# A SwiGLU kernel whose first loads are dealt anew over two DMA queues, with ScalarE's table load ahead of its own

## The chip, the core and the metric

The kernel runs on one core of one Trainium2 chip. The metric is the device time of one execution in microseconds (us). Before the change, three timed runs took 120.75, 120.0 and 120.8 us, median 120.75. One further execution was profiled.

Five engines appear in what follows. TensorE (PE) does matmuls; its weight loads have a row of their own (PEld). VectorE (DVE), ScalarE (ACT) and GpSimd (POOL) do elementwise work. SyncE (SP) here only issues DMAs and waits. DMAs can be issued by SyncE and by ScalarE; each of the two has a queue of its own (q1 and q10 in the profile).

## What is computed

```
def reference(x, w_gate, w_up, w_down):
    g = _silu(x @ w_gate)
    u = x @ w_up
    return (g * u) @ w_down
```

All arrays are bfloat16: x is 1 x 2048 x 512 (tokens by D), w_gate and w_up are 512 x 1376 (D by F), w_down is 1376 x 512.

## The kernel before

The work has two phases. In the first, for each chunk of 512 tokens and each of the ten full tiles of 128 columns of F, PE computes a gate group and an up group (`gu_matmuls`, four matmuls each over D = 4 x 128); ScalarE applies SiLU to the gate group in PSUM and VectorE multiplies it with the up group. The 96 columns that are left over go through groups of their own (X and Y). In the second phase PE multiplies the result with w_down, ScalarE and VectorE copy it out of PSUM, and SyncE stores it.

PE needs x with D on the partitions (`xT_sb`). Tokens 0 to 255 of the first chunk come as plain loads (`load_xn`, tiles xn0 and xn1 of 128 tokens) and are transposed on PE (line 367); VectorE and ScalarE copy the transposes to `xT_sb` in turn (even and odd parts of D). Tokens 256 to 511 come by two DMA transposes (x0b, x0c), and the later chunks by one each (x1 to x3). The weights come in slabs of tiles: tile 0, tile 1, tiles 2-3, tiles 4-6, tiles 7-10, each with a load for gate (wg0, wg1, wg2, wg4, wg7) and one for up (wu0 ... wu7). "Ups 2-3" below is the load wu2.

The order of all this is written out by hand. Each engine has one stream of instructions; a DMA issue is an instruction in the stream of the engine that issues it, and each load has a semaphore of its own. ScalarE's stream (`on_scalar`) begins with gate 0 and xn1, then a dummy SiLU on four elements (line 277), ahead of which the program has a load of ScalarE's function table; then come its real operations, of which the first are copies of the transposes. SyncE's stream (`on_sync`) issues xn0, up 0, gate 1, up 1, gates 2-3, ups 2-3, x0b, x0c, and then all the rest.

PE's stream begins with seven matmuls on constants (`warm`: five of 512 columns and two of 128). Behind them stand:

- the four transposes of xn0, two more matmuls on constants, and gate tile 0 on tokens 0-127;
- the four transposes of xn1, up tile 0 on tokens 0-127, and gate and up tile 0 on tokens 128-255;
- tiles 1, 2 and 3 on tokens 0-255 in the order gate 1, up 1, gate 2, gate 3, up 2, up 3, as matmuls of 256 columns;
- tile 0 on tokens 256-383 and then on 384-511, tiles 1 to 3 on tokens 256-511, and from tile 4 on whole chunks of 512 columns.

Each waits for the semaphores of the loads that it uses (`need`) and for the copies (`after`).

Of the kernel before, what the change touches and what calls it, by code (L numbers as in the profile page):

```python
# [4 lines left out]
ACT = mybir.ActivationFunctionType  # L5
# [9 lines left out]
def bass_standalone__swiglu_ffn__prompt_kernel(nc, x, w_gate, w_up, w_down, out):  # L15
# [35 lines left out]
    with ExitStack() as es:  # L51
# [11 lines left out]
        adummy = sb("act_dummy", [P, 8], FP32)  # L63
# [21 lines left out]
        def load_sem(name):  # L85
            loads[name] = sem(f"s_{name}")
            return loads[name]
# [3 lines left out]
        zero_c = nc.const_aps.tensor(0.0, [P, 4], FP32)  # L91


        def load_x(eng, name, t0, t1):
            eng.dma_start_transpose(
                xT_sb[:, :, t0:t1], xf[t0:t1, :]
            ).then_inc(load_sem(name), 16)

        def load_w(eng, name, src, base, f0, f1):
            eng.dma_start(  # L100
                w_sb[:, :, base + f0:base + f1],
                src[:, f0:f1].rearrange("(k p) f -> p k f", p=P),
            ).then_inc(load_sem(name), 16)

        slabs = [(0, 1), (1, 2), (2, 4), (4, 7), (7, NFT)]
        slab_of = {ft: a for a, b in slabs for ft in range(a, b)}

        def load_gate(eng, a, b):
            load_w(eng, f"wg{a}", w_gate, 0, a * P, min(b * P, F))

        def load_up(eng, a, b):
            load_w(eng, f"wu{a}", w_up, UPH, a * P, min(b * P, F - 32))

        def load_xn(eng, i):
            eng.dma_start(xn_sb[:, i, :], xf[i * P:(i + 1) * P, :]).then_inc(load_sem(f"xn{i}"), 16)
# [2 lines left out]
            return of[t * P:(t + 1) * P, :]  # L118

        def loads_on_scalar(act):  # L120
            load_gate(act, *slabs[0])
            load_xn(act, 1)

        def loads_on_sync(sp):
            load_xn(sp, 0)
            load_up(sp, *slabs[0])
            for a, b in slabs[1:3]:
                load_gate(sp, a, b)
                load_up(sp, a, b)
            load_x(sp, "x0b", HT, HT + P)  # L130
            load_x(sp, "x0c", HT + P, SC)
            for a, b in slabs[3:]:
                load_gate(sp, a, b)
                load_up(sp, a, b)
            load_w(sp, "wut", w_up, F - (F - 32), F - 32, F)
            for c in range(1, NSC):
                load_x(sp, f"x{c}", c * SC, (c + 1) * SC)
            sp.dma_start(
                wd_sb[:, 0:NFF, :], w_down[0:NFF * P, :].rearrange("(k p) d -> p k d", p=P)
            ).then_inc(load_sem("wd"), 16)  # L140
            load_sem("wdt")
            for y0 in (0, 64):
                sp.dma_start(wd_sb[y0:y0 + 64, T01, :], w_down[NFF * P:F - SR, :]).then_inc(loads["wdt"], 16)
            for x0 in range(0, P, SR):
                sp.dma_start(wd_sb[x0:x0 + SR, T2, :], w_down[F - SR:F, :]).then_inc(loads["wdt"], 16)
            sp.dma_start(wd_sb[0:F_LAST, TAIL, :], w_down[NFF * P:F, :]).then_inc(load_sem("wdl"), 16)
# [104 lines left out]
        def ready(op):  # L251
            return op["ready"] if "ready" in op else (s_P, op["g"]["at"] + 1)

        def store_tiles(eng, own):
            for o, t, c0, c1, ob, copied, n in stores:
                if o == own:
                    eng.wait_ge(s_A if copied == "A" else s_D, n)
                    eng.dma_start(out_rows(t)[:, c0:c1], o_sb[ob][:, c0:c1]).then_inc(s_out[ob], 16)

        def on_sync(sp):  # L260
            loads_on_sync(sp)
            store_tiles(sp, "S")
            for i in range(NOS):
                sp.wait_ge(s_out[i], 16 * n_store[i])
# [9 lines left out]

        def on_scalar(act):
            loads_on_scalar(act)
            act.activation(adummy[:, 0:4], zero_c, ACT.Silu)  # L277
            for op in act_ops:
                act.wait_ge(*ready(op))
                if op["kind"] == "silu":  # L280
                    if op["free"]:
                        act.wait_ge(s_D, op["free"])
                    fn = ACT.Silu
                else:
                    if op["stored"][1]:
                        act.wait_ge(*op["stored"])
                    fn = ACT.Copy
                act.activation(op["out"], op["src"], fn).then_inc(s_A, 1)  # L288
            store_tiles(act, "A")
# [199 lines left out]
        on_sync(nc.sync)  # L489
        on_gpsimd(nc.gpsimd)  # L490
        on_scalar(nc.scalar)
        on_tensor(nc.tensor)
        on_vector(nc.vector)
# [28 lines left out]
```

## Time and profile before

| What | Value |
|---|---|
| timed runs | 120.0, 120.75, 120.8 us (median 120.75) |
| profiled execution, its time | 120.41 us |
| profiled execution, its span | 119.1 us, 2344 instructions |
| PE busy | 116.5 us, 98% of the span |
| VectorE, ScalarE busy | 38.3 and 35.2 us (32% and 30%) |
| DMA queue q1 (SyncE) | 16816 packets, 8.33 MB |
| DMA queue q10 (ScalarE) | 816 packets, 0.36 MB |

The span is the time from the first to the last instruction of the program in the profile; the execution's own time has 1.3 us more around it. In the lines shown further on, "0.74 0.46 ACTq L100 DMA_DIRECT2D w_sb<-in_w_gate_dram x1" means: at 0.74 us of the span the instruction stream of ScalarE issued a DMA for 0.46 us, by line 100, from w_gate to w_sb. A q behind an engine's name marks its instruction stream. In the table of DMA issues the last column is the time from the issue to the landing of the data. In the chain of waits each line has a start, a length, and the engine, tile and line that the chain goes through. PE's matmuls overlap each other, so the pace is read from their starts.

### The profile page before, as it was taken

The page shows a single profiled execution, that of the slowest core. Times are in us where ns is not written, and L with a number is a line of the kernel's source. Part 1 is how long each engine was busy: PE and PEld are TensorE (multiplying, and loading weights), DVE is VectorE, ACT ScalarE, POOL GpSimd, SP SyncE. Part 2 cuts the span into 40 slices and gives each one's busy share as a digit, 9 for nine tenths or more (in the row PEclk, how much of TensorE's full clock was granted, in tenths as well). Part 3 has the DMA queues.
Part 4 walks back from the last instruction along what each step waited for, and adds up shares of the span by engine and source line. Part 5 has one row for each costly group of instructions (what it writes and reads, how often), then busy time and mean ns, then how long its engine had stood idle before and what let it go on. Part 6 is the DMA issues. An engine that isn't in the chain of part 4 may idle for free.

```text
span 119.1 us, 2344 instructions
## 1 busy us (share of the span) xinstructions
PE 116.5 (98%) x1019; PEld 60.6 (51%) x1019; DVE 38.3 (32%) x61; ACT 35.2 (30%) x62; POOL 1.0 (1%) x7
## 2 busy tenths in 40 slices
PE   7999999999999999999999999999999999999993
PEld 2899544444444444444444444444444445885452
DVE  0204633444334444334453344361000044003321
ACT  3406444262343272442353432430000033003021
POOL 1000000000000000000000000001000000000000
DMA  4999989991000000000000000000000017200612
GB/s 84 296 176 347 265 178 239 265 340 29 0 6 0 0 0 0 0 6 0 0 0 6 0 0 0 0 0 6 0 6 0 0 51 235 77 0 6 204 61 88
DMA packets 17642, 8.83 MB, mean 74 GB/s; under 512 B 10624, under 2 KB 17632, under 8 KB 17632
## 3 DMA queue, kind: packets, MB, share of 16 engines
q1 hardware_dynamic: 16816, 8.33, 27.5%
q10 hardware_dynamic: 816, 0.36, 1.1%
q8 instruction: 8, 0.13, 0.4%
q14 instruction: 2, 0.02, 0.1%
HBM read 4.75 MB, written 2.10 MB: 58 GB/s over the span
## 4 chain that ended last, share of the span: by engine, by line
PE 98%; DVE 0%; issue 0%
PE bank L326 62%; PE bank L444 25%; PE bank L483 7%; PE bank L358 2%; PE bank L406 2%; PE bank L367 1%; DVE o_sb L302 0%
## 5 line engine op out<-in xcount | busy, mean ns | idle before, releaser
L326 PE MATMUL bank<-xT_sb,w_sb 128*128 128x512 bf16 (+2 forms) x384 | 73.7, 356 | 0.0
L326 PEld LDWEIGHTS bank<-xT_sb,w_sb 128*128 128x128 bf16 x384 | 37.0, 100 | 36.3
L298 DVE TENSOR_TENSOR hT_sb<-sg_sb,bank 128x512 bf16<-128x512 f32 x40 | 27.5, 687 | 40.5 <-PE bank L326 39.6
L288 ACT ACTIVATE sg_sb<-bank 128x512 f32<-128x512 f32 x40 | 23.8, 596 | 40.9 <-PE bank L326 40.8
L444 PE MATMUL bank<-wd_sb,hT_sb 32*128 32x512 bf16 x496 | 29.0, 374 | 0.0
L444 PEld LDWEIGHTS bank<-wd_sb,hT_sb 32*128 32x128 bf16 x496 | 15.2, 93 | 11.6 <-issue 0.4
L302 DVE CAST o_sb<-bank 128x512 bf16<-128x512 f32 (+1 forms) x10 | 5.7, 595 | 31.1 <-PE bank L444 25.9
L288 ACT ACTIVATE o_sb<-bank 128x512 bf16<-128x512 f32 (+1 forms) x8 | 4.3, 582 | 33.6 <-PE bank L444 27.9
L483 PE MATMUL bank<-wd_sb,hT_sb 128*128 128x512 bf16 (+2 forms) x56 | 8.1, 304 | 0.0
L483 PEld LDWEIGHTS bank<-wd_sb,hT_sb 128*128 128x128 bf16 x56 | 4.2, 97 | 4.2 <-issue 0.4
L444 PE MATMUL bank<-wd_sb,hy_sb 32*128 32x512 bf16 (+1 forms) x32 | 5.0, 371 | 0.0
L298 DVE TENSOR_TENSOR hx_sb<-sgx_sb,bank 32x512 bf16<-32x512 f32 x4 | 2.8, 692 | 3.5 <-ACT sgx_sb L288 3.5
L288 ACT ACTIVATE sgx_sb<-bank 32x512 f32<-32x512 f32 x4 | 2.3, 587 | 4.5 <-PE bank L326 4.5
L358 PE MATMUL bank<-const-bfloat16-1.0 128*128 128x512 bf16 (+1 forms) x9 | 2.9, 486 | 0.8 <-PEq L507 0.8
L444 PE MATMUL bank<-wd_sb,hx_sb 32*128 32x512 bf16 (+1 forms) x16 | 3.0, 371 | 0.0
L288 ACT ACTIVATE sgy_sb<-bank 64x512 f32<-64x512 f32 x4 | 2.4, 590 | 0.1
L358 PEld LDWEIGHTS bank<-const-bfloat16-1.0 128*128 128x128 bf16 x9 | 1.1, 140 | 2.1 <-issue 2.1
L406 PE MATMUL bank<-xT_sb,w_sb 128*64 128x512 bf16 x16 | 1.9, 382 | 0.0
L444 PEld LDWEIGHTS bank<-wd_sb,hy_sb 32*128 32x128 bf16 x32 | 1.6, 93 | 0.6
L302 DVE COPY xT_sb<-bank 128x128 bf16<-128x128 bf16 x4 | 0.9, 224 | 3.0 <-PE bank L367 3.0
L277 ACT ACT_TABLE_LOAD x1 | 1.3, 1283 | 1.8 <-issue 1.8
L406 PEld LDWEIGHTS bank<-xT_sb,w_sb 128*64 128x64 bf16 x16 | 0.8, 109 | 1.0 <-DVE hT_sb L298 0.4
(16 smaller groups left out, 7.3 us busy)
## 6 DMA issues: line engine op xcount, KB each, us to landing
out_dram<-o_sb SPq DMA_DIRECT2D x15, 128.0 KB, 1.8
wd_sb<-in_w_down_dram SPq DMA_DIRECT2D x1, 1280.0 KB, 8.3
w_sb<-in_w_gate_dram SPq DMA_DIRECT2D x1, 480.0 KB, 5.5
w_sb<-in_w_up_dram SPq DMA_DIRECT2D x1, 448.0 KB, 7.5
w_sb<-in_w_gate_dram SPq DMA_DIRECT2D x1, 384.0 KB, 4.0
w_sb<-in_w_up_dram SPq DMA_DIRECT2D x1, 384.0 KB, 4.4
w_sb<-in_w_up_dram SPq DMA_DIRECT2D x2, 128.0 KB, 3.3
w_sb<-in_w_gate_dram SPq DMA_DIRECT2D x1, 256.0 KB, 3.7
```

The lines of the kernel that those rows point to most:

```text
L277: act.activation(adummy[:, 0:4], zero_c, ACT.Silu)
L288: act.activation(op["out"], op["src"], fn).then_inc(s_A, 1)
L298: ins = dve.tensor_tensor(op["out"], op["a"], op["b"], ALU.mult)
L302: ins = dve.tensor_copy(op["out"], op["src"])
L326: return pe.matmul(bank[:, n0:n1], lhsT=w_sb[:, dk, col:col + P], rhs=xT_sb[:, dk, c * SC + n0:c * SC + n1], start=(dk == 0), stop=(dk == ...
L358: pe.matmul(banks[NB - 1][:, 0:width], lhsT=ones_w, rhs=ones_m[:, 0:width], start=True, stop=True)
L367: pe.matmul(tview(i, dk), lhsT=xn_sb[:, i, dk * P:(dk + 1) * P], rhs=ident[:, :], start=True, stop=True, is_transpose=True,).then_inc(s_X, 1)
L406: ins = pe.matmul(g["bank"][y0:y1, :], lhsT=w_sb[:, dk, YC0:YC0 + 64], rhs=xT_sb[:, dk, c * SC:(c + 1) * SC], start=(dk == 0), stop=(dk == ...
L444: ins = pe.matmul(g["bank"][:, 0:c1 - c0], lhsT=h, rhs=wd_sb[r0:r0 + SR, w, c0:c1], start=(start and fk == fks[0]), stop=(stop and fk == f ...
L483: ins = pe.matmul(g["bank"][:, 0:c1 - c0], lhsT=h, rhs=w, start=(last and fk == 0), stop=(fk == (NFF if last else NFF - 1)), skip_group_ch ...
```

## The change

ScalarE's dummy SiLU, with its table load, moves to the head of ScalarE's stream. Behind it, ScalarE issues gate 0 and xn1 as before, and now also up 1 and ups 2-3, which leave SyncE's stream. SyncE's order becomes xn0, up 0, gate 1, gates 2-3, x0b, x0c, and the rest as before. PE's, VectorE's and GpSimd's streams are the same.

```diff
         def loads_on_scalar(act):
+            act.activation(adummy[:, 0:4], zero_c, ACT.Silu)
             load_gate(act, *slabs[0])
             load_xn(act, 1)
+            for a, b in slabs[1:3]:
+                load_up(act, a, b)
 
         def loads_on_sync(sp):
             load_xn(sp, 0)
             load_up(sp, *slabs[0])
             for a, b in slabs[1:3]:
                 load_gate(sp, a, b)
-                load_up(sp, a, b)
             load_x(sp, "x0b", HT, HT + P)
             load_x(sp, "x0c", HT + P, SC)
...
         def on_scalar(act):
             loads_on_scalar(act)
-            act.activation(adummy[:, 0:4], zero_c, ACT.Silu)
             for op in act_ops:
```

## The prediction

> **What bounds the kernel now.** I read the page's parts 1 and 4 first, then the chain of waits cut to the first 12 us, the timeline of the loading stage, the table of DMA issues, and the windows. The chain of the whole span:
>
> ```profile
> PE 98%; DVE 0%; issue 0%
> ```
>
> TensorE (PE) is the path from 0.77 us to the end. The change touches only loads that land in the first 9 us, so what counts is whether PE waits for one of them. The chain of the first 12 us:
>
> ```profile
> 0.77 2.51 PE bank L358 x7
> 3.28 0.01 issue
> 3.29 0.58 PE bank L367 x4
> 3.88 0.21 PE bank L358 x2
> 4.09 0.46 PE bank L326 x4
> 4.55 0.47 PE bank L367 x4
> 5.01 7.01 PE bank L326 x73
> ```
>
> The seven warm-up matmuls fill the time until the first tokens (xn0) are there; then the work follows without a hole. What it follows on is seen from the issues (start, length of the issue) and from the time that each takes to land:
>
> ```profile
> 0.74 0.46 ACTq L100 DMA_DIRECT2D w_sb<-in_w_gate_dram  x1
> 0.74 0.40 SPq L115 DMA_DIRECT2D xn_sb<-in_x_dram  x1
> ...
> 1.23 0.53 ACTq L115 DMA_DIRECT2D xn_sb<-in_x_dram  x1
> ...
> 1.79 1.28 ACT L277 ACT_TABLE_LOAD   x1 [1.79 <-issue]
> ...
> 2.75 0.51 SPq L100 DMA_DIRECT2D w_sb<-in_w_gate_dram  x1
> ...
> 3.08 0.20 ACT L277 ACTIVATE act_dummy<-const-float32-0.0 128x4 f32<-128x4 f32 x1
> ...
> 3.30 0.51 SPq L100 DMA_DIRECT2D w_sb<-in_w_up_dram  x1
> ...
> 3.85 2.64 SPq L95 DMA_TRANSPOSE xT_sb<-in_x_dram  x2
> ```
>
> ```profile
> w_sb<-in_w_gate_dram SPq DMA_DIRECT2D x1, 256.0 KB, 3.7
> w_sb<-in_w_up_dram SPq DMA_DIRECT2D x1, 256.0 KB, 3.9
> w_sb<-in_w_gate_dram ACTq DMA_DIRECT2D x1, 128.0 KB, 2.9
> xn_sb<-in_x_dram SPq DMA_DIRECT2D x1, 128.0 KB, 2.4
> xn_sb<-in_x_dram ACTq DMA_DIRECT2D x1, 128.0 KB, 3.1
> ```
>
> Issue plus time to land gives the arrivals; beside them, from narrow cuts of PE's timeline, the first matmul that needs each. xn0: 0.74 + 2.4 = 3.1, used 3.29. Gate 0: 0.74 + 2.9 = 3.6, used 3.96 (set by the copies of the transposes, of which ScalarE's first starts at 3.70). xn1: 1.23 + 3.1 = 4.3, used 4.41: this one is only just in time. Gate 1: 1.66 + 3.4 = 5.1, used 6.06. Up 1: 2.20 + 3.3 = 5.5, used 6.50. Gates 2-3: 2.75 + 3.7 = 6.45, used 6.93. Ups 2-3: 3.30 + 3.9 = 7.2, used 7.81. Tokens 256-383 and 384-511: 7.9 and 8.3, used 8.68 and 9.13. So every load that the change moves is early by 0.5 to 1.0 us, and only xn0 and xn1 are on the path. One more thing is in these starts: up to 5.98 a 128-column matmul follows the last after 0.107 us, from 8.68 on after 0.056. PE runs at half pace for its first 5.2 us (0.77 to 5.98) and at full pace behind that. The granted clock in the windows stands at 1.00 in both, so the pace is read from the starts.
>
> **The change, part by part.** The sum is made against the profiled execution: span 119.1, time 120.41. The shown median is 120.75, so 0.34 above it; I add the same steps to both.
>
> (1) Table load and dummy SiLU ahead of ScalarE's two loads. They are 1.28 + 0.20 us of ScalarE's own work. The question is whether the instruction stream behind them, which now begins with four DMA issues, has to wait. Lower bound: only two instructions more to hand over. The nearest rows are two semaphore instructions of ScalarE 0.087 us apart (109.248 and 109.335), and SyncE's 0.05 to 0.06 between the end of an issue and the next; so 0.12 to 0.2 for both. Upper bound: all of 1.28 to 1.49. Two rows bear on it. The trace has the semaphore instruction at 109.335, which belongs to the copy that starts at 113.26, before the preceding copy has begun (109.74) and while the one before that runs (109.24 to 109.84): the stream goes on while the engine works. And the dummy starts 0.01 us after the table load's end (1.79 + 1.28 = 3.07, then 3.08), while VectorE shows 0.044 from a released semaphore instruction to the start of the work behind it: the dummy had been handed over while the table was loading. Both rows are of engine instructions and none is of a DMA behind a table load, so it stays a rival; I take the lower bound, 0.15. [...]
>
> With 0.15, gate 0 lands at 3.75, still ahead of 3.96: hidden by the copies, cost 0. xn1 lands near 4.5, so its transposes go from 4.41 to about 4.55. That is 0.15 of half-pace time; if full pace still comes at 5.98, the work left over runs twice as fast, so 0.07 to 0.15. I take 0.1. Against this, xn0 has the DMA engines to itself a little longer; it can gain at most 3.29 - 3.08 = 0.2 (where the warm-up ends), and I keep -0.1 as the lower end of this part.
>
> (2) Ups 1 and 2-3 leave SyncE's queue for ScalarE's. SyncE's later issues, gates 2-3 and all behind, come 0.55 earlier, from the tokens on 1.10 earlier (two issues of 0.51 with their gaps). Nothing waits for that: the tokens were 0.8 early. ScalarE issues four times, about 0.5 us each, from 0.9 to 3.1, and its next work is the copy at 3.70: cover of 0.6. The bytes to move by 7.2 are unchanged, and the DMA engines already run full then (286 to 303 GB/s in the windows 5:6 and 6:7). What changes is who shares: the two queues have 640 KB each up to gates 2-3 and ups 2-3, and at half the rate each they end about together, instead of at 6.45 and 7.2. Gates 2-3 are needed at 6.93. Bounds: 0, if their queue is ahead by the 0.15 of part (1) and by xn0's head start; 7.2 - 6.93 = 0.3, if they land only with ups 2-3. I take 0.05, near the lower end, because the head start is some 60 KB of 640 and the matmuls have moved back by 0.1 as well.
>
> (3) The table load is over at 2.0 and not 3.07. ScalarE's first real work waits for PE until 3.70; worth 0.
>
> Sum: +0.1 + 0.05 = +0.15: 120.56 against the profiled time, 120.9 against the median. Own range: -0.1 to +0.45, so 120.65 to 121.2, and with the runs' own spread (120.0 to 120.8) 120.0 to 121.3.
>
> **Rivals.** Rival 1, slower: the DMA issues wait for the table load. It decides as soon as ScalarE's first issue is later than about 0.74 + (3.96 - 3.6) = 1.1 us. Place: PE before its first real matmul. First issue 0.74 + 1.28 = 2.03, at most 2.24. Gate 0 lands at 2.03 + 2.9 = 4.9 to 5.1, xn1 1.3 to 1.5 late at 5.6 to 5.8. PE idles from 3.88 to 5.0 and again until 5.7. The four ScalarE copies come late too (issues until 4.2), behind gate 0. What it costs depends on the pace. If full pace still comes at 5.98: by then the old kernel had 1.57 us of half-pace time since 4.41, worth 0.79 at full pace; the new one has 0.28, worth 0.14; plus up to 0.1 for copies. That makes +0.7. If the idle time starts the 5.2 us of half pace anew at 5.0 to 5.6, full pace comes at 10.2 to 10.8; 5.2 us from 5.6 are then worth 2.6, against 0.79 + 4.8 = 5.6 in the old kernel: +3.0. So 121.1 to 123.4 against the profiled time, 121.45 to 123.75 against the median, middle 122.6. For it: no row shows a DMA of ScalarE behind a table load. Against it: the two rows of part (1). Chance 0.44, high for that evidence because everything hangs on one unseen order of two instructions, and the slack is 0.1 to 0.4 us.
>
> Rival 2: the tokens' transposes, 1.10 earlier, run between ups 2-3 of the other queue. Where transposes and copies follow each other now, the DMA engines slow down: 156 and 80 GB/s in the windows 7:8 and 8:9, against 286 in 6:7. If ups 2-3 land with the tokens at 8.3, PE waits 8.3 - 7.81 = 0.5: 121.3 against the median. Against it: at 6 to 7 us the two kinds overlap already, at 286 GB/s. Chance 0.06.
>
> Rival 3: xn0's gain of 0.1 to 0.2 outweighs the rest, 120.6. Against it: xn1 is the next to be waited for. Chance 0.05.
>
> **How the numbers follow.** My forecast, that the order on ScalarE costs next to nothing and the rest is hidden, has 0.45; predicted time 120.9. The range goes from the lowest run, 120.0, to 123.0, which takes in all but rival 1's upper quarter or so (0.13) and a little below (0.03). A measurement of this kernel tells about 1% from no change: below 119.55 or above 121.95. Rival 1 lies above that but for its lower fifth or so (0.37 of 0.44), rival 2 with 0.01: slower 0.38. Faster by 1% would need 1.2 us out of a PE that has only 0.2 us of waits in its head; 0.03 is left for it. The rest, 0.59, is within 1%.
>
> **What would show it.** Step (1) is right if ScalarE's first DMA issue stands near 0.9 while the table load still runs, and wrong if it stands at 2.0 or later. Step (2) is right if PE's first 256-column matmul stands near 6.1 and the chain has no wait at gates 2-3, near 7.0. Step (3) shows in ScalarE's first copy, still near 3.7. The prediction is wrong if PE has a hole between 3.9 and 5.7, and by how much is seen from the time at which the spacing falls from 0.107 to 0.056.

## The result, and the profile after

The changed kernel takes 120.97 us (median of 22 runs, 120.42 to 123.09). In the same series the kernel before takes 120.44 (22 runs, 119.94 to 120.8). The ratio is 1.0049, 95% interval 1.0034 to 1.0064: about 0.6 us slower, inside the 1% that was called "no change", and clear of zero. One of the changed kernel's 22 runs (123.09) was a slow one, and the ratios here and below leave slow runs out.

The profiled execution of the changed kernel has a span of 119.8 us and a time of 121.1. The chain of waits over the whole span no longer begins with PE (columns: start, length, what):

```profile
0.74 0.39 SPq L115
...
1.19 0.42 SPq L100
...
1.66 0.50 SPq L100
...
2.21 5.33 DMA w_sb<-in_w_gate_dram
7.54 0.05 issue
7.58 71.05 PE bank L327 x360
78.63 1.85 PE bank L407 x16
80.48 29.41 PE bank L445 x540
109.89 8.06 PE bank L484 x58
```

The path to the end now goes through one load, gates 2-3: issued by SyncE at 2.21, landed at 7.54, first matmul at 7.58. Behind that, nothing has changed: from the first matmul on gate 2 to the end of the span it is 112.18 us here (119.767 - 7.585) and 112.15 before (119.081 - 6.933). So the whole difference lies ahead of this matmul. PE's timeline there (the bracket gives idle time before the group and what ended it):

```profile
3.91 0.51 PE L327 MATMUL bank<-xT_sb,w_sb 128*128 128x128 bf16 x4
4.71 0.40 PE L368 MATMUL bank<-ident,xn_sb 128*128 128x128 bf16 x4 [0.29 <-DMA xn_sb<-in_x_dram]
4.94 0.94 PE L327 MATMUL bank<-xT_sb,w_sb 128*128 128x128 bf16 x12
6.15 1.06 PE L327 MATMUL bank<-xT_sb,w_sb 128*128 128x256 bf16 x8 [0.27 <-DMA w_sb<-in_w_gate_dram]
7.58 0.61 PE L327 MATMUL bank<-xT_sb,w_sb 128*128 128x256 bf16 x4 [0.38 <-DMA w_sb<-in_w_gate_dram]
```

PE waits three times: for xn1, for gate 1 and for gates 2-3. In this execution full pace came early, between 4.19 and 4.71 us (5.98 in the profile before), which gave PE time that it then spent waiting. Over all profiles here full pace comes anywhere from about 4.2 to 6.5, so the starts of two single profiles are not quite like with like. The fastest runs tell more: the fastest of 22 took 119.94 before and 120.42 after, so the best case moved by nearly as much as the median did. ScalarE's timeline shows the part that the prediction was least sure of:

```profile
0.74 1.28 ACT L121 ACT_TABLE_LOAD   x1 [0.74 <-PEq L508]
0.81 0.44 ACTq L100 DMA_DIRECT2D w_sb<-in_w_gate_dram  x1
1.28 0.53 ACTq L115 DMA_DIRECT2D xn_sb<-in_x_dram  x1
1.84 0.46 ACTq L100 DMA_DIRECT2D w_sb<-in_w_up_dram  x1
2.04 0.20 ACT L121 ACTIVATE act_dummy<-const-float32-0.0 128x4 f32<-128x4 f32 x1
2.32 0.53 ACTq L100 DMA_DIRECT2D w_sb<-in_w_up_dram  x1
```

The DMA issues run on while the table load (0.74 to 2.02) is under way, the first of them 0.07 us behind its start. The table of DMA issues tells where the time went instead (last column: from issue to landing):

```profile
w_sb<-in_w_gate_dram SPq DMA_DIRECT2D x1, 256.0 KB, 5.3
w_sb<-in_w_up_dram ACTq DMA_DIRECT2D x1, 256.0 KB, 5.8
...
xn_sb<-in_x_dram ACTq DMA_DIRECT2D x1, 128.0 KB, 3.4
w_sb<-in_w_gate_dram SPq DMA_DIRECT2D x1, 128.0 KB, 4.4
w_sb<-in_w_up_dram ACTq DMA_DIRECT2D x1, 128.0 KB, 4.7
```

Gates 2-3 are issued 0.54 earlier and take 5.3 us instead of 3.7. Gate 1 takes 4.4 instead of 3.4, up 1 4.7 instead of 3.3, ups 2-3 5.8 instead of 3.9. In landings: gate 1 6.10 (5.03 before), up 1 6.54 (5.47), gates 2-3 7.54 (6.43), ups 2-3 8.13 (7.21).

A load's semaphore gets 16 increments in the trace (those of gates 2-3 come from 5.73 to 6.43 before and from 5.72 to 7.54 after), and PE waits for the last of them. The trace has the time of each and names no DMA engine with it. For gates 2-3 the eighth comes at 6.00 before and 6.50 after, the last at 6.43 and 7.54. So the eighth is 0.5 later, and the last falls back by another 0.6. The DMA engines together move little less than before: 225 GB/s against 273 from 4 to 5 us, then 314 and 291 against 303 and 286 in the two windows behind it.

### The profile page after: what moved, and what is told of

It reads as the page before. It is cut to its first block, busy times and chain, and to the rows that moved or that the text cites. A ratio compares the mean times of both kernels' runs of the same rounds, so it can differ in the third digit from the quotient of the medians.

```text
span 119.8 us, 2344 instructions
## 1 busy us (share of the span) xinstructions
PE 116.2 (97%) x1019; PEld 59.7 (50%) x1019; DVE 38.3 (32%) x61; ACT 35.1 (29%) x62; POOL 1.0 (1%) x7
## 4 chain that ended last, share of the span: by engine, by line
PE 92%; DMA 4%; SPq 1%; issue 0%; DVE 0%
PE bank L327 59%; PE bank L445 25%; PE bank L484 7%; DMA w_sb<-in_w_gate_dram 4%; PE bank L407 2%; SPq L100 1%; SPq L115 0%; DVE o_sb L303 0%
## 5 line engine op out<-in xcount | busy, mean ns | idle before, releaser
L327 PEld LDWEIGHTS bank<-xT_sb,w_sb 128*128 128x128 bf16 x384 | 36.1, 98 | 37.6 <-DMA w_sb<-in_w_gate_dram 1.1
L289 ACT ACTIVATE xT_sb<-bank 128x128 bf16<-128x128 bf16 x4 | 0.9, 276 | 2.3 <-PE bank L368 2.3
```

The lines of the kernel that those rows point to most:

```text
L327: return pe.matmul(bank[:, n0:n1], lhsT=w_sb[:, dk, col:col + P], rhs=xT_sb[:, dk, c * SC + n0:c * SC + n1], start=(dk == 0), stop=(dk == ...
```

## The experiments

The theory with which they were begun, an assumption of the author's at that point: both queues share the DMA engines, so ups on ScalarE's queue take a share from the gates on SyncE's that PE uses sooner (sharing). Rivals: the table load (T), the tokens' transposes, issued earlier (X), two busy queues as such (Q), and a cost for any load that is moved (S). Each kernel's ratio is to the kernel before on the same chip. "Eighth" is the eighth of the 16 increments of gates 2-3 (in the run with halves the 16th of 32), "start" the first matmul on gate 2, "rest" the span less that start. The run with wide loads, whose gates come in one load, is told in its own section. All but the ratio are from one profile each.

| Kernel | ratio, 95% interval | gate 1 lands | gates 2-3: eighth, last | start | rest |
|---|---|---|---|---|---|
| before | 1 | 5.03 | 6.00, 6.43 | 6.93 | 112.15 |
| the change | 1.0049 (1.0034 to 1.0064) | 6.10 | 6.50, 7.54 | 7.58 | 112.18 |
| table load first, alone | 0.9999 (0.9982 to 1.0015) | 5.05 | 6.10, 6.35 | 6.52 | 112.15 |
| ups moved, alone | 1.0040 (1.0021 to 1.0060) | 5.26 | 6.23, 6.85 | 7.22 | 112.17 |
| halves on both queues | 1.0010 (0.9993 to 1.0028) | 5.40 | 5.84, 6.50 | 7.07 | 112.16 |
| transposes wait for xn1 | 1.0030 (1.0014 to 1.0047) | 5.77 | 6.35, 7.25 | 7.29 | 112.16 |
| transposes wait for gates 2-3 | 1.0202 (1.0187 to 1.0218) | 6.05 | 6.43, 7.44 | 7.49 | - |
| only up 1 moved | 1.0025 (1.0007 to 1.0044) | 5.67 | 6.13, 6.75 | 7.35 | 112.15 |
| only gate 1 moved | 1.0049 (1.0023 to 1.0074) | 6.64 | 6.35, 6.92 | 7.57 | 112.16 |
| only ups 2-3 moved | 1.0083 (1.0055 to 1.0111) | 5.74 | 7.62, 7.65 | 7.69 | 112.17 |
| mirrored: gates moved | 1.0090 (1.0064 to 1.0116) | 6.42 | 7.67, 7.87 | 7.91 | 112.17 |
| 928 KB more beside | 1.0328 (1.0281 to 1.0376) | 6.79 | 8.70, 9.50 | 9.55 | 113.66 |
| xn1 sooner | 1.0007 (0.9990 to 1.0023) | 5.25 | 6.23, 6.51 | 6.56 | 112.18 |

### The table load first, alone

```diff
         def loads_on_scalar(act):
+            act.activation(adummy[:, 0:4], zero_c, ACT.Silu)
             load_gate(act, *slabs[0])
             load_xn(act, 1)
...
             loads_on_scalar(act)
-            act.activation(adummy[:, 0:4], zero_c, ACT.Silu)
```

> The kernel before with the dummy SiLU and its table load moved ahead of ScalarE's two loads, and nothing else. Theory (the cost is the two queues' sharing of the DMA engines once the ups go to ScalarE): ScalarE's first DMA issue stands at 0.81 us while the table load runs, gates 2-3 land near 6.4 as before, PE does not wait for them, ratio to the kernel before 0.998 to 1.002. Rival T (the table load delays gate 0 and xn1, and all behind): xn1 lands at 4.5 or later, PE waits 0.1 to 0.3 us ahead of its transposes, ratio 1.002 to 1.005. Rival X (the tokens' transposes, issued earlier, slow the other loads): as the theory, since SyncE's order is unchanged.

Ratio 0.9999, ScalarE's first issue at 0.80, gates 2-3 at 6.35. PE does wait for xn1, as rival T said, and the chain of its first 13 us shows it:

```profile
0.73 0.50 ACT L121
1.23 0.03 issue
1.26 3.30 DMA xn_sb<-in_x_dram
4.57 0.05 issue
4.61 0.43 PE bank L367 x4
```

But the time is the same. xn1 was on the path before too (4.36, used 4.41), and 0.2 us of waiting there is within what the runs spread (119.97 to 120.72). T falls as a cause.

### The ups moved, alone

```diff
             load_gate(act, *slabs[0])
             load_xn(act, 1)
+            act.activation(adummy[:, 0:4], zero_c, ACT.Silu)
+            for a, b in slabs[1:3]:
+                load_up(act, a, b)
```

(with SyncE's side as in the change)

> The changed kernel with the dummy SiLU behind ScalarE's gate 0 and xn1 and ahead of its two ups: the ups' move alone. Theory: gates 1 and 2-3 land near 6.1 and 7.5 (5.0 and 6.4 in the kernel before), the first matmul on gate 2 starts near 7.6, ratio 1.003 to 1.007, the whole of the change. Rival T: ratio within 1.002 of 1. Rival X: as the theory, since the transposes are issued near 2.8 here too.

Ratio 1.0040: the ups' move is the change's cost, within the intervals all of it. Its fastest run is 120.45, against 119.77 for the kernel before on this chip. The profiled execution (120.71) stands in the middle of its runs (median 120.72), but it does not show the path that was expected: gates 2-3 land at 6.85, 0.7 ahead of the 7.5 that was expected, and PE, at half pace until about 6.4, comes to them without a wait at 7.22. So the ratio shows what the move costs; where this kernel loses the time, its one profile does not show.

### Halves on both queues

```diff
-            for a, b in slabs[1:3]:
-                load_up(act, a, b)
+            for a, b in slabs[1:3]:
+                load_half(act, a, b, 2)
...
-            for a, b in slabs[1:3]:
-                load_gate(sp, a, b)
+            for a, b in slabs[1:3]:
+                load_half(sp, a, b, 0)
```

(`load_half(eng, a, b, k0)` loads parts k0 and k0+1 of D, first of the gate slab, then of the up slab)

> The changed kernel, but gate 1, up 1, gates 2-3 and ups 2-3 are each loaded in two halves (two of the four parts of D each), one from each queue, in the order gate, up, gates, ups on both. Both queues are as busy as in the changed kernel, and the loads come in the order in which PE uses them. Theory (what costs is that ups take the gates' share): gates 1 lands near 5.2, gates 2-3 near 6.6, ratio 0.998 to 1.003. Rival Q (two busy queues are slower as such: engines out of step, rate lower): gates 2-3 land at 7.2 or later, ratio 1.003 to 1.007. Rival X: SyncE's transposes come as late as in the kernel before here (six issues ahead of them), so ratio near 1 as well.

Ratio 1.0010, gates 2-3 at 6.50, eighth at 5.84. The queues carry as many bytes as in the change, but both carry the gates first. That takes back most of the cost. So two busy queues by themselves cost 0.28% at most, by this interval (Q falls as the main cause); what counts is what stands beside what. The transposes are issued at 3.74 here, near the 3.85 of the kernel before, so this run alone does not part sharing from X.

### The transposes later

Two kernels, the changed one with one line each ahead of SyncE's x0b:

```diff
+            sp.wait_ge(loads["xn1"], 16)
             load_x(sp, "x0b", HT, HT + P)
```

```diff
+            sp.wait_ge(loads["wg2"], 16)
             load_x(sp, "x0b", HT, HT + P)
```

> The changed kernel, but SyncE waits until xn1 has landed (near 4.6) before it issues the DMA transposes of tokens 256 to 511 (2.8 in the changed kernel, 3.9 in the kernel before). Theory (sharing): gate 1 lands near 6.1 as in the changed kernel, gates 2-3 near 7.3, PE still waits 0.4 us or more for them, ratio 1.003 to 1.007; the tokens land near 8.7 and 9.1. Rival X: gates 2-3 land near 6.5 to 6.8, ups 2-3 near 7.2, ratio 0.999 to 1.002.

> The changed kernel, but SyncE waits until gates 2-3 have landed before it issues the transposes of tokens 256 to 511, so that no transpose is under way while the weights of tiles 1 to 3 come. PE may then wait for the tokens, whose landing follows gates 2-3 by a fixed time; the median over the runs still tells when gates 2-3 land: its distance from the profiled run's time is added to the profiled landing. Theory (sharing): landing by that reckoning 7.1 to 7.7, ratio to the kernel before above 1.005. Rival X (the transposes, earlier than before, hold the copies up): landing 6.3 to 6.7.

With the first, the transposes are issued at 4.49, later than in the kernel before (3.85). The ratio is 1.0030, its interval overlaps the change's, and gates 2-3 still land at 7.25. With the second, nothing of the tokens is under way, and the chain of its first 13 us still has

```profile
2.20 5.24 DMA w_sb<-in_w_gate_dram
7.44 0.02 issue
7.46 1.29 SPq L95
8.75 0.05 issue
8.80 2.71 DMA xT_sb<-in_x_dram
```

PE waits for the tokens there, so the ratio says nothing by itself. But the median (122.67) is 0.21 below the profiled time (122.88), which puts gates 2-3 at 7.23 in the middle of the four runs, if the way from their landing to the end takes the same time in each: sharing's 7.1 to 7.7, and not X's 6.3 to 6.7. The profile itself has 7.44. X falls as the main cause. A part of some 0.2% is left open by the first of the two.

### One load moved at a time

Only up 1, only ups 2-3, and, as a counterpart, only gate 1 on ScalarE's queue:

```diff
             load_xn(act, 1)
+            load_up(act, *slabs[1])      # only up 1
+            load_up(act, *slabs[2])      # only ups 2-3
+            load_gate(act, *slabs[1])    # only gate 1
```

(one of the three lines each, with the same load taken out of SyncE's order)

> The changed kernel, but only up 1 goes to ScalarE's queue; ups 2-3 stay with SyncE behind gates 2-3. Theory (a load that is used later takes the engines' share from one that is used sooner): up 1 stood ahead of gates 2-3 anyway, so these land near 6.5 as before; only gate 1 comes later, near 5.4, which is used near 5.7 to 6.1. Ratio to the kernel before 0.999 to 1.002. Rival S (moving any load to the second queue costs, by its issue or by engines out of step): half of the change's cost, 1.002 to 1.003, gates 2-3 near 7.

> The changed kernel, but only ups 2-3 go to ScalarE's queue; up 1 stays with SyncE ahead of gates 2-3. Theory: the 256 KB of ups 2-3 run beside gate 1, up 1 and gates 2-3 and take bytes from them; gates 2-3 land near 7.0 to 7.4, ratio 1.003 to 1.006, most of the change's cost. Rival S: as much as with up 1 alone, 1.002 to 1.003.

> The counterpart of the run with up 1 alone on ScalarE (1.0025): gate 1, the load that PE uses first, goes to ScalarE's queue behind xn1, and up 1, gates 2-3 and ups 2-3 stay on SyncE in that order. Two queues, one load moved, the same bytes. Theory (what is used sooner must not share): gate 1 and up 1 share, so gate 1 lands between 5.0 and 5.5 and up 1 near 5.4, gates 2-3 near 6.4; ratio 0.999 to 1.002. Rival S (any load moved costs): 1.002 to 1.003.

All three missed the theory's ranges; up 1 alone fell into rival S's. Up 1 alone costs 1.0025, gate 1 alone 1.0049 and ups 2-3 alone 1.0083, by its middle more than both ups together (the intervals touch).

With up 1 alone, the profile has no wait at gate 1 or at gates 2-3. Its path goes through xn1, which lands at 4.81 (4.36 before), and full pace comes only at about 6.4:

```profile
1.26 3.55 DMA xn_sb<-in_x_dram
4.81 0.05 issue
4.86 0.61 PE bank L369 x4
```

So xn1, the last load that ScalarE issues ahead of up 1, is a second place where a moved load can cost; one profile does not show more than that.

With gate 1 alone, the two loads that share, gate 1 and up 1, both come late: 6.64 and 6.07, against 5.03 and 5.47 where they follow each other on one queue. PE has a hole of 0.3 us ahead of gate 1, and the chain goes through it:

```profile
1.84 4.80 DMA w_sb<-in_w_gate_dram
6.64 0.05 issue
6.68 6.52 PE bank L328 x65
```

Sharing in its plain form, by which only the order matters, doesn't say that: the last of two loads that share should land no later than the second of two in a row. Two things are seen beside it. The last increments come late (the eighth of gate 1 at 5.58, the last at 6.64), and the engines move less from 4 to 5 us (176 GB/s, 273 before). So S is right that each of these three moves costs, though not in the amounts. It does not hold for every move: with xn1 sooner, below, up 0 goes to ScalarE's queue at no cost that is clear of zero.

With ups 2-3 alone, gates 2-3 stand behind up 1 on SyncE and are the last of the weights. Their 16 increments come all within 7.59 to 7.65, just ahead of the tokens (8.15 to 8.25). In the kernel before it is ups 2-3, the last load ahead of the transposes, whose increments come together (7.15 to 7.21), while those of gates 2-3 are spread over 5.73 to 6.43. In these kernels it is the load issued last ahead of the transposes' bytes whose increments come close together, on whichever queue it is: in the changed kernel it is ups 2-3 on ScalarE's (7.80 to 8.13). Single packets of the trace bunch as well. In the changed kernel nine packets of 4 bytes on SyncE's queue start between 6.62 and 7.17, last up to 1.02 us and all end at 7.64 to 7.66, 0.2 behind the end of the last 512-byte packet (7.47). Before, seven of them end at 7.07, 0.2 behind 6.87; with no transposes under way none lasts over 0.01. In the kernel before, the load whose increments come together is one which PE uses at 7.81; with ups 2-3 alone moved it is one that PE is waiting for:

```profile
2.76 4.89 DMA w_sb<-in_w_gate_dram
7.65 0.05 issue
7.69 5.33 PE bank L328 x55
```

In the run without transposes under way the increments of ups 2-3 do not bunch (6.57 to 7.80). What makes all 16 come so late and so close together is not shown.

### Mirrored

```diff
-            for a, b in slabs[1:3]:
-                load_up(act, a, b)
+            for a, b in slabs[1:3]:
+                load_gate(act, a, b)
...
-                load_gate(sp, a, b)
+                load_up(sp, a, b)
```

> The change mirrored: gates 1 and 2-3 go to ScalarE's queue and ups 1 and 2-3 stay on SyncE; the table load is first as in the changed kernel. Theory (sharing, whichever queue the gates are on): gates 1 lands near 5.7 and gates 2-3 near 7.2 as in the changed kernel, ratio 1.003 to 1.006. Rival (SyncE's queue is the one that suffers, because the transposes stand behind the gates there): gates land as in the kernel before, ratio within 1.002.

Ratio 1.0090, above the range. It makes no difference in sign which queue the gates are on. Gates 2-3 are issued last of the four here (2.31) and land bunched (15 increments from 7.64 to 7.70, the last at 7.87), as with ups 2-3 alone; by the ratios this is the worse place for them.

### More beside

```diff
         def loads_on_scalar(act):
+            act.activation(adummy[:, 0:4], zero_c, ACT.Silu)
             load_gate(act, *slabs[0])
             load_xn(act, 1)
+            load_gate(act, *slabs[4])
+            load_up(act, *slabs[4])
```

(taken from SyncE, where they stood behind the tokens)

> The kernel before with the table load first (which alone did not change the time) and with the last slab's gate and up, tiles 7 to 10, 928 KB that are needed only after 17 us, moved from SyncE to ScalarE's queue right behind xn1: a larger dose of the same thing. Theory: SyncE's loads get half of the DMA engines from 2.5 us on; gates 2-3 have some 520 KB of SyncE's bytes ahead of them and with them behind 2.5 us, at half of 300 GB/s lands them near 8 to 9.5, and the span is longer by the same amount by which the first matmul on gate 2 is later; ratio 1.012 to 1.03. If the queues take turns by packet and not by byte, ScalarE's packets of 960 B against 256 B take more than half: gates 2-3 later than 10, ratio above 1.03. Rival S (no dependence on the bytes beside): ratio 1.003 to 1.005.

Ratio 1.0328, gates 2-3 at 9.50: they land in the theory's range, and the larger dose costs more, slightly more than the range. The table of the DMA queues for 5 to 7 us shows how the engines are shared (columns: packets, MB, share of the 16 engines):

```profile
q10 hardware_dynamic: 561, 0.51, 77.8%
q1 hardware_dynamic: 575, 0.14, 32.1%
```

Nearly equal numbers of packets, but ScalarE's are of 960 and 896 B and SyncE's of 256 B, so ScalarE's queue gets 0.51 MB and SyncE's 0.14. With ups 2-3 alone (512 B against 256 B) it is 0.17 MB against 0.13 between 4.5 and 5.5 us, with 336 against 500 packets: more bytes for the longer packets there too, but not packet for packet.

The rest of the span is 1.5 us longer than in the other kernels of the table, where the theory had it unchanged. The windows tell why (columns: window, its length and PE's busy time with the matmuls, granted clock, DMA share, GB/s):

```profile
7.00:9.55 2.55, 1.05 (x8) 0.93 1.35 336
9.55:12.50 2.95, 2.95 (x14) 0.50 1.08 276
12.50:20.00 7.50, 7.45 (x61) 0.99 1.13 215
```

PE is granted half its clock for 2.95 us, which is worth the 1.5. The one of its runs whose clock stayed at 1.00 took 123.15. Ahead of the fall stand three holes of 0.69, 1.04 and 0.45 us, between 6.1 and 9.55. What brings the fall is not shown: one hole of 1.41 us with the wide loads, and 1.5 us of holes between 9.20 and 11.55 where the transposes wait for gates 2-3, leave the clock at 1.00 behind them. In the profile of the change three holes add up to 0.9 us within 3.2, and the clock stays at 1.00 too.

### Two versions meant to be faster

```diff
# wide
-        slabs = [(0, 1), (1, 2), (2, 4), (4, 7), (7, NFT)]
+        slabs = [(0, 1), (1, 4), (4, 7), (7, NFT)]
...
-            for at in (2, 3, 4, 6, 5, 7):
+            for at in (2, 4, 6, 3, 5, 7):
# xn1 sooner
             load_gate(act, *slabs[0])
-            load_xn(act, 1)
+            load_up(act, *slabs[0])
...
             load_xn(sp, 0)
-            load_up(sp, *slabs[0])
+            load_xn(sp, 1)
```

> The kernel before, with tiles 1 to 3 in one gate and one up load of 384 KB each instead of two and two, both on SyncE, and PE's order gates 1, 2, 3, ups 1, 2, 3: the loads that PE waits for in fewer and longer pieces. Theory: the end of all six tiles' loads decides; with packets of 768 B they land near 5.4 (gates) and 6.5 (ups), ups used near 6.6; ratio 0.997 to 1.0. Rival: the gates as a whole land too late for tile 1 (after 5.7), ratio 1.001 to 1.004.

> A version made after the traces, which put xn1 on the path: the kernel before, with xn1 second on SyncE and up 0 second on ScalarE (exchanged). Theory: xn1 lands near 3.9 instead of 4.4, its transposes follow gate 0's matmuls without a wait, up 0 lands near 4.4, just before it is used; PE is 0.2 to 0.4 us further at the tile 1 matmuls, and gains that where full pace comes late; where it comes early, gates 2-3 at 6.4 stop it. Ratio 0.996 to 0.9995. Rival: up 0 is now the late one, 0.999 to 1.002.

The wide loads cost: ratio 1.0046 (1.0020 to 1.0071). The gates of tiles 1 to 3 land at 7.24, though 15 of their 16 increments are there by 6.12, and PE stands still from 5.87 to 7.28:

```profile
1.66 5.58 DMA w_sb<-in_w_gate_dram
7.24 0.05 issue
7.28 5.76 PE bank L326 x59
```

The last increment again, and here without a second busy queue at that time. From 6.9 to 7.96 the only packets of the weights are 0.036 us long and one behind the other, and from 7.3 to 7.9 no other bytes move beside them.

With xn1 sooner it lands at 3.93, and PE goes into its transposes without a hole. The ratio is 1.0007 (0.9990 to 1.0023): no gain. The chain of the first 13 us shows who is next:

```profile
2.68 3.83 DMA w_sb<-in_w_gate_dram
6.51 0.05 issue
6.56 6.51 PE bank L326 x61
```

Gates 2-3 again, at 6.51. No version beat the kernel before.

## Why the prediction was right in its number and wrong in a step

**Step 1, the table load: right.** The lower bound held, and by more than was taken: the first issue is 0.07 us behind the table load's start and not 0.15, and alone the step costs nothing (0.9999). The +0.1 that the sum has for it did not show. Rival 1, with 0.44 the largest, did not happen; the two rows against it (the semaphore instruction between two copies, and the 0.01 us ahead of the dummy) had pointed the right way. The issue at 0.81 lies inside the load's 0.74 to 2.02. PE does have a hole between 3.9 and 5.7, which the prediction named as a sign against it: 0.29 us ahead of xn1's transposes at 4.71. It is not rival 1's, since the issues did not wait. xn1 landed at 4.66, where the prediction had 4.5, and with full pace early PE came to it sooner.

**Step 2, the ups' move: wrong in size.** It was put at 0.05, with 0.3 as the upper end. The moved ups alone cost 0.40% (0.5 us), and in the profile of the change gates 2-3 land 1.11 later, with the wait in the chain that the prediction had named as a sign against this step. What failed is the sentence "the bytes to move by 7.2 are unchanged", from which it followed that the last load would land at 7.2 at the worst. The bytes are unchanged, and from 5 to 7 us the engines move them as fast as before (314 and 291 GB/s against 303 and 286), but PE waits for the last of a load's 16 increments, and that of gates 2-3 fell further behind the eighth (1.04 us, 0.43 before). Ups 2-3 landed at 8.13 and gates 2-3 at 7.54, both behind the supposed worst case. The prediction did name sharing and gates 2-3 as the place.

**Step 3: right.** ScalarE's first copy stands at 3.64.

**The sum.** 120.9 against a measured 120.97 looks better than it is. It was 120.75, the median of three runs, plus 0.15. The longer series has 120.44 plus 0.53. A base 0.3 too high made up for most of a step 0.4 too small: that is luck. The cost of 0.53 lies outside the prediction's own -0.1 to +0.45 for the change alone.

**Rivals 2 and 3.** Rival 2 (transposes between the ups) has a likeness in the bunched increments, but in the change these are those of ups 2-3, which PE uses at 8.47 and which land at 8.13: no wait there. They are the next in line, though: had gates 2-3 been on time, with ups 2-3 used at 7.81 as before, PE would have waited for them for some 0.3 us, an estimate from these two times. Held back to 4.49, the transposes still left the ratio at 1.0030. Rival 3's gain at xn0 was 0.06 (first transpose at 3.23, not 3.29), and xn1 ate it, as said against it.

**What stays open.** Why the last increment falls behind the eighth, by 0.4 us in the kernel before, 1.0 in the change and 1.6 with wide loads (1.1 of it behind the fifteenth), is not shown: the trace gives each increment's time and names no engine with it. That the share is lost to the other queue is shown by the halves (1.0010, the change 1.0049) and by the dose (1.0328, with 0.51 of 0.65 MB on the other queue), and the run without transposes under way has the gates late all the same (7.44). That the lag grows with the sharing is seen in single profiles only, and the wide loads have it without a second queue. The costs of the loads moved one at a time do not follow from sharing alone.

## What to carry to other kernels

Where several loads are waited for in turn, put them on one queue in the order of their use; in this kernel a second queue let a load that is used later take bytes from one that is used sooner (1.0049, against 1.0010 with both queues in the order of use), and earlier issue did not help: gates 2-3 were issued 0.54 us sooner and landed 1.11 later. Read the slack of a load to its last increment, not to the mean: a slack of 0.5 us was used up by the increments behind the eighth (6.50, the last 7.54). A dummy activation that loads the function table stood ahead of ScalarE's DMA issues at no cost that could be measured here (0.9999).

## What was not expected of the hardware

- ScalarE issued DMAs while its table load ran (0.81 in 0.74 to 2.02).
- The load issued last ahead of the DMA transposes' bytes had its 16 increments close together (within 0.06 us, 7.15 to 7.21, before; within 0.33 in the change) where those of gates 2-3 spread over 0.7 and 1.8. In front of them 4-byte packets lasted up to 1.02 us and ended together, 0.2 behind the last 512-byte packet.
- With packets of 960 and 896 B against 256 B the two queues moved 561 and 575 packets in 2 us, so the longer packets took 0.51 of 0.65 MB.
- With 928 KB more beside, PE's granted clock was 0.50 for 2.95 us behind holes of which none was over 1.04 us; behind one hole of 1.41 us (wide loads) it stayed at 1.00.
